# Weights staged through several buffers and idle slots, x loaded a block ahead, the second output product split by k among the next block's columns

## The chip, the cores and the metric

One core of one Trainium2 chip runs the kernel. The metric is the device time of one execution in microseconds (us); lower is better. TensorE is called PE, VectorE DVE, ScalarE ACT, GpSimd POOL and SyncE, which issues every DMA here, SP.

## The reference

A recurrent attention gives `x` (batch 4, 768 positions, 320 features). Two mixtures follow, and they are what the change touches:

```python
def _moe_ref(x, w_in, g_ln, w_sg, b_sg, w_out):
    h = gelu_tanh(x @ w_in)                      # 320 -> 1024
    u, v = h[..., :512], h[..., 512:]
    v_n = (v - mean(v)) / sqrt(var(v) + 1e-06) * g_ln
    v_s = einsum('ts,bsd->btd', w_sg, v_n) + b_sg[None, :, None]   # 768 x 768
    return x + (u * v_s) @ w_out                 # 512 -> 320
def _moe2_ref(x, w_in, conv_w, w_out):
    h = maximum(x @ w_in, 0)                     # 320 -> 1024
    conv_out = three taps of conv_w over the positions of h
    return (h * sigmoid(conv_out)) @ w_out       # 1024 -> 320
```

`w_in` and `w_out` of both mixtures and `conv_w` arrive as 64-bit floats, `w_sg` and the vectors as 32-bit ones.

## The kernel before, in words

`everything` runs `attention`, which writes `x` to a DRAM tensor transposed (features by positions), then `moe`, then a flag that says whether a fallback has to run (it does not here). A scheduler with a timeline of its own turns the order in which the code is written into one order of instructions for each engine; engines run theirs strictly in order. A tile pool gives each name (or tag) a number of buffers, and whoever wants a buffer anew waits until the last reader of the old tile is done.

Every product is made in three terms from a high and a low half of each operand (hi·hi, hi·lo, lo·hi). So each weight is staged: `convert` (L435) loads a piece into the tile `raw` (one buffer, L444), rebuilds 32-bit floats from the 64-bit words with one ACT and four DVE operations into `wq` and `wt` (L448 to L458, which share the tag `vv` with four buffers), and `halves` (L461) writes the high half on ACT and the low half on POOL. `weight_in` (L466) does this in six pieces, left half of the 1024 columns first, `weight_out` (L478) in pieces of 128 rows, `weight_sg` (L509) in six 384 KB pieces that go through the same one buffer.

A block is one batch and one half of the positions, 384 of them; there are eight. First mixture:
- `in1(b, c)` (L522) loads the block's x into `x2t`, splits it into `xh` and `xl`, makes `ph` (the v half, 24 matmuls, L539), gelu, mean and variance and the normalised `vh`, `vl` (L542 to L564), and `pu` (the u half, 32 matmuls, L570).
- `sg(b, c)` (L575) multiplies the `vh`, `vl` of both blocks of a batch by `w_sg`: four groups of 18 matmuls (L588), each finished by DVE `g`, POOL times u, ACT `gh`, DVE `gl`.
- `out1(b, c)` (L600) is the output product, 36 matmuls (L609), written in among the groups of the next `sg`.

They are called in the order of L613 to L628: `in1(0,0)`, all of w_sg, all of w_out, `in1(0,1)`, and then the loop over batches; the second mixture's two weights are staged behind the loop, into the places of the first's (`win_hi`, `big_hi` and their low halves, one buffer each).

Second mixture, after all eight blocks: `in2(i, f)` (L647) makes one of eight columns of 128 hidden features (8 matmuls, L656), and then a chain: ACT relu into `hz` (L657) and first tap into `cv` (L659), DVE the two other taps (L660, L662), ACT sigmoid (L664), POOL times h (L665), ACT `gh` (L668), DVE `gl` (L669). `cv` has two buffers. `out2(i, tt)` (L672) makes one of three groups of 128 positions of the output: 24 matmuls (L679) over all eight columns, evicted by ACT (L682). The loop (L687) writes the three `out2` of block i-1 between the fourth and the fifth column of block i, and the last block's at the end.

Of the kernel before, what the change touches and what calls it, by code (L numbers as in the profile page):

```python
# [10 lines left out]
F32 = mybir.dt.float32  # L11
# [408 lines left out]
def moe(ctx, tc, ident, gy, x, w_in, g_ln, w_sg, b_sg, w_out, w_in2, conv_w, w_out2, out):  # L420
    nc = tc.nc
    B, DM, S = x.shape
    FF = w_in.shape[1]
# [11 lines left out]
    def convert(parts, dst_hi, dst_lo):  # L435

        n = dst_hi.shape[-1]
        m = slice(0, dst_hi.shape[0])
        if parts[0][1].dtype == F32:
            w = work.tile([128, 512], F32, name="raw", bufs=1)  # L440
            for rows, src in parts:
                nc.sync.dma_start(out=w[rows, 0:n], in_=src)
            return halves(w[m, 0:n], dst_hi, dst_lo)
        raw = work.tile([128, 512, 2], U32, name="raw", bufs=1)  # L444
        for rows, src in parts:
            nc.sync.dma_start(out=raw[rows, 0:n], in_=src.bitcast(U32).rearrange("p (n t) -> p n t", t=2))
        low, high = raw[m, 0:n, 0], raw[m, 0:n, 1]
        q = work.tile([128, 512], F32, name="wq", tag="vv", bufs=4)[m, 0:n]  # L448
        t = work.tile([128, 512], U32, name="wt", tag="vv", bufs=4)[m, 0:n]
# [16 lines left out]
    def weight_in(src, name):  # L466

        hi = wpool.tile([128, 3, FF], F32R, name=f"{name}_hi", tag="win_hi")
        lo = wpool.tile([128, 3, FF], F32R, name=f"{name}_lo", tag="win_lo")
        for c in range(0, FF, 512):  # L470
            f = slice(c, c + 512)
            for k in range(3):
                parts = [(slice(0, 128), src[128 * k:128 * k + 128, f])] if k < 2 else \
                    [(slice(0, TAIL), src[256:DM, f]), (slice(64, 128), src[256:DM, f])]
                convert(parts, hi[:, k, f], lo[:, k, f])
        return hi, lo

# [41 lines left out]
    with tc.tile_pool(name="m_u", bufs=9) as pool_u, tc.tile_pool(name="m_wo", bufs=1) as pool_wo:  # L519
        wo = {}  # L520

        def in1(b, c):  # L522
# [6 lines left out]
            xh = work.tile([128, 3, N2], F32R, name="xh", bufs=1)  # L529
            xl = work.tile([128, 2, N2], F32R, name="xl", bufs=1)  # L530
# [44 lines left out]
        def sg(b, c, prev):  # L575
# [3 lines left out]
            for f in range(NF1):  # L579
# [46 lines left out]
        w2_hi, w2_lo = weight_in(w_in2, "w2")  # L626
        out1(*prev)
        v_hi, v_lo = weight_out(wpool, w_out2, NF2, "wv", "big", False)  # L628

    with tc.tile_pool(name="m_g", bufs=2) as pool_g:  # L630
# [16 lines left out]
        def in2(i, f, xh, xl):  # L647
# [10 lines left out]
            cv = work.tile([128, N2], F32, name="cv")  # L658
# [7 lines left out]
            gh = pool_g.tile([128, N2], F32R, name="gh2", bufs=12)  # L666
            gl = pool_g.tile([128, N2], F32R, name="gl2", bufs=12)
# [4 lines left out]
        def out2(i, tt, gs):  # L672
            b, c = divmod(i, 2)
            po = ps_o.tile([128, DM], F32, name="pq", tag="po")
            ts = slice(128 * tt, 128 * tt + 128)
            n = 0
            for g, rr in ((0, v_hi), (0, v_lo), (1, v_hi)):
                for k in range(NF2):
                    nc.tensor.matmul(out=po, lhsT=gs[k][g][:, ts], rhs=rr[:, k], start=(n == 0), stop=(n == 3 * NF2 - 1))  # L679
                    n += 1  # L680
# [88 lines left out]
```

## Time and profile before

| | us |
|---|---|
| median of 3 runs | 1226.54 (1223.62 to 1234.17) |
| span of the profiled execution | 1226.1 |
| PE busy in it | 862.2 (70%) |
| DVE busy | 729.2 (59%) |
| ACT busy | 429.0 (35%) |
| POOL busy | 229.8 (19%) |

The profiled execution has a span of 1226.1 us and stands some 0.4 us under the median of the runs. Attention takes the first 684 us. Busy shares are averages over stages with different limits, so they are read by stretch.

### The profile page before, as it was taken

The numbers are of one execution on the slowest core, as the hardware profiler recorded it, in microseconds if no ns is written. First come the engines' busy times: TensorE is split into PE (matmuls) and PEld (weight loads), VectorE is DVE, ScalarE is ACT, GpSimd is POOL, SyncE is SP. The second block draws the span as 40 slices with busy tenths as digits, with TensorE's granted clock in tenths as the row PEclk, the third lists the DMA queues.
The fourth block names the chain that finished last, engine by engine and source line by source line (L and its number), as shares of the span: only waits on it lengthen the run. The fifth ranks groups of instructions, "written<-read, shape, count | busy, mean of one in ns | idle before, by whom it ended". The sixth has DMA issues, their size and how long they took to land.

```text
span 1226.1 us, 23366 instructions
## 1 busy us (share of the span) xinstructions
PE 862.2 (70%) x9777; PEld 798.7 (65%) x9777; DVE 729.2 (59%) x1348; ACT 429.0 (35%) x833; POOL 229.8 (19%) x217
## 2 busy tenths in 40 slices
PE   2207652973867488296789056599999977999895
PEld 2207642763756477285678045499999966999894
DVE  6573277459459637935932334775555668667663
ACT  2204211321332241133133133232333246767663
POOL 5212010011010201101000023121111424323321
PEclk9657785977879688687989669799999988999997
DMA  9712260244154242413301732100000221000000
GB/s 159 135 33 40 43 113 22 59 78 105 27 106 90 58 75 57 97 44 53 71 22 27 204 118 63 50 1 1 1 1 1 69 71 32 32 18 18 17 32 20
DMA packets 102786, 69.33 MB, mean 57 GB/s; under 512 B 83600, under 2 KB 89744, under 8 KB 101520
## 3 DMA queue, kind: packets, MB, share of 16 engines
q1 hardware_dynamic: 102672, 67.75, 24.9%
q8 instruction: 79, 1.29, 0.5%
q14 instruction: 35, 0.29, 0.1%
HBM read 59.86 MB, written 7.86 MB: 55 GB/s over the span
## 4 chain that ended last, share of the span: by engine, by line
PE 41%; DVE 25%; DMA 16%; issue 6%; ACT 6%; POOL 3%; SPq 1%; DVEq 0%; POOLq 0%; ACTq 0%
PE pv L588 6%; PE gk L124 4%; DVE mtmp L168 3%; PE pr L609 3%; DVE mu L170 3%; PE pq L679 3%; DMA raw<-in_moe_w_in 3%; DMA at<-in_c_a 3%; PE pu L570 3%; PE ph L539 3%; DMA w<-in_c_wp 2%; PE pzt L252 2%; PE gh L276 2%; PE p L656 2%; DMA raw<-in_moe_w_out 2%
## 5 line engine op out<-in xcount | busy, mean ns | idle before, releaser
L189 PE MATMUL pn<-tn,la 32*32 32x32 f32 x768 | 18.9, 214 | 156.9 <-DVE tn L174 155.7
L189 PEld LDWEIGHTS pn<-tn,la 32*32 32x32 f32 x768 | 17.5, 129 | 159.3 <-issue 156.8
L124 PE MATMUL gk<-at,kbt 128*128 128x128 f32 x384 | 68.8, 330 | 45.2 <-POOL kbt L102 31.8
L124 PEld LDWEIGHTS gk<-at,kbt 128*128 128x128 f32 x384 | 60.2, 236 | 48.6 <-POOL kbt L102 32.2
L102 POOL TENSOR_TENSOR kbt<-kbt,w 128x1024 f32<-128x1024 f32 x24 | 55.5, 2330 | 166.6 <-DMA w<-in_c_wp 61.9
L665 POOL TENSOR_TENSOR cv<-cv,hz 128x384 f32<-128x384 f32 x64 | 60.7, 955 | 130.6 <-ACT cv L664 130.6
L100 DVE SCALAR_TENSOR_TENSOR at<-at,px 64x512 f32<-64x512 f32 x48 | 42.3, 916 | 65.8 <-DMA at<-in_c_a 59.7
L168 DVE TENSOR_TENSOR mtmp<-mu 128x30 f32<-128x30 f32 (+9 forms) x180 | 67.0, 372 | 5.0
L170 DVE TENSOR_TENSOR mu<-mu,mtmp 128x30 f32<-128x30 f32 (+9 forms) x180 | 64.8, 360 | 5.0
L539 PE MATMUL ph<-wi_hi,xh 128*128 128x512 f32 x72 | 24.0, 435 | 62.3 <-ACT wi_hi L462 40.0
L588 PE MATMUL pv<-sg_hi,vh 128*128 128x384 f32 x192 | 64.5, 336 | 0.6 <-ACT vh L562 0.6
L588 PE MATMUL pv<-sg_lo,vh 128*128 128x384 f32 x192 | 64.5, 336 | 0.0
L207 ACT ACTIVATE la<-at 64x1024 f32<-64x1024 f32 x24 | 25.2, 1052 | 110.4 <-PE pn L189 63.2
L588 PE MATMUL pv<-sg_hi,vl 128*128 128x384 f32 x192 | 63.8, 336 | 0.0
L592 POOL TENSOR_TENSOR g<-g,u 128x384 f32<-128x384 f32 x32 | 35.5, 1112 | 138.9 <-DVE g L591 136.6
L679 PE MATMUL pq<-wv_hi,gh 128*128 128x320 f32 x192 | 43.8, 334 | 23.9 <-ACT gh L668 23.9
L135 POOL COPY la<-la 32x512 f32<-32x512 f32 x24 | 14.6, 608 | 241.9 <-DVE la L127 219.7
L285 PE MATMUL pyo<-r,s 128*64 128x64 f32 x704 | 57.3, 248 | 3.1 <-ACT n L195 1.9
L280 DVE TENSOR_TENSOR ghs<-gh,mask 128x512 f32<-128x512 f32 x48 | 32.7, 681 | 44.5 <-PE gh L276 26.7
L539 PEld LDWEIGHTS ph<-wi_hi,xh 128*128 128x128 f32 x72 | 14.3, 207 | 67.6 <-ACT wi_hi L462 40.6
L287 PE MATMUL pyo<-ghs,kbn 128*64 128x64 f32 x768 | 57.5, 241 | 0.0
L127 DVE TENSOR_TENSOR la<-gk,mask 128x512 f32<-128x512 f32 x48 | 33.0, 687 | 41.3 <-PE gk L124 41.2
(151 smaller groups left out, 2463.7 us busy)
## 6 DMA issues: line engine op xcount, KB each, us to landing
kbt<-in_c_kb SPq DMA_DIRECT2D x24, 384.0 KB
w<-in_c_wp SPq DMA_DIRECT2D x48, 130.0 KB
w<-in_c_wr SPq DMA_DIRECT2D x48, 130.0 KB
zv<-in_c_vt SPq DMA_DIRECT2D x48, 128.0 KB
at<-in_c_a SPq DMA_DIRECT2D x24, 192.0 KB
r<-in_c_r SPq DMA_DIRECT2D x48, 96.0 KB
raw<-in_moe_w_in SPq DMA_DIRECT2D x8, 512.0 KB
vz<-in_c_v SPq DMA_DIRECT2D x24, 160.0 KB
```

The lines of the kernel that those rows point to most:

```text
L100: nc.vector.scalar_tensor_tensor(out=at[half[P], ns, P], in0=at[half[P], ns, P], scalar=-1.0, in1=px[half[P], ns, 0:C], op0=ALU.mult, op1= ...
L102: nc.gpsimd.tensor_tensor(out=kbt[:, ns], in0=kbt[:, ns], in1=w2[:, :, C - 1::-1][:, :, None, :].to_broadcast([128, 8, 2, C]), op=ALU.mult)
L124: nc.tensor.matmul(out=pg[:, j].rearrange("p P t -> p (P t)"), lhsT=kbt[:, n].rearrange("p c t -> p (c t)"), rhs=at[:, n].rearrange("p P t ...
L168: nc.vector.tensor_tensor(out=tv, in0=mu[:, j + 1:32, j:j + 1].to_broadcast([128, n, j]), in1=mu[:, j:j + 1, 0:j].to_broadcast([128, n, j] ...
L170: nc.vector.tensor_tensor(out=mu[:, j + 1:32, 0:j], in0=mu[:, j + 1:32, 0:j], in1=tv, op=ALU.add)
L285: nc.tensor.matmul(out=pyo[half[P], i], lhsT=s0s[hg, q][:, D * i:D * i + 64], rhs=r2[:, i, P], start=True, stop=False)
L287: nc.tensor.matmul(out=pyo[half[P], i], lhsT=kbn[:, 8 * q + i, P], rhs=ghs[:, j, P], start=(hg == 0), stop=True)
L539: nc.tensor.matmul(out=po, lhsT=xx[:, k, 128 * i:128 * i + 128], rhs=ww[:, k, FH:FF], start=(n == 0), stop=(n == len(ps) - 1))
L570: nc.tensor.matmul(out=po, lhsT=ww[:, k, 128 * f:128 * f + 128], rhs=xx[:, k], start=(n == 0), stop=(n == len(ps) - 1))
L588: nc.tensor.matmul(out=po, lhsT=l[:, fs], rhs=rr[:, k, cs], start=(n == 0), stop=(n == 3 * NT - 1))
L665: nc.gpsimd.tensor_tensor(out=cv, in0=cv, in1=h[:, 1:N2 + 1], op=ALU.mult)
L679: nc.tensor.matmul(out=po, lhsT=gs[k][g][:, ts], rhs=rr[:, k], start=(n == 0), stop=(n == 3 * NF2 - 1))
```

## The change

- The load of a piece (`load`) is parted from its conversion. `raw` has two buffers; the pieces of `w_in` alternate between these and the two buffers of `u`, which are idle then; `w_sg` goes in twelve half pieces through the twelve buffers of `gh` and `gl`.
- `weight_in` takes the right half of the columns (the one that `ph` needs) first.
- The loads of x become `in1_x`, called one block ahead of the block's `in1`.
- `in1(0,1)` is written ahead of the staging of `w_sg` and `w_out`; the second mixture's `conv_w` and `w_in` are staged ahead of the last batch's `sg` instead of behind it.
- `out2` takes one column k (9 matmuls into three accumulators) and is written behind each `in2` of the next block; a new `finish2` evicts the three accumulators. `gh2`, `gl2` go from 12 to 16 buffers.
- `xh`, `xl`, `g`, `gh`, `gl`, the `wo` halves, `cv` and `xt` move to other pools; `g` has two buffers instead of three.

```diff
+    def load(parts, n, pool, bufs, tags):
+
+        if len(parts[0][1]) == 1:
+            w = pool.tile([128, n], F32, name="wst", tag=tags[0], bufs=bufs)
+            for rows, (src,) in parts:
+                nc.sync.dma_start(out=w[rows], in_=src)
+            return [w]
+        raw = pool.tile([128, 512, 2], U32, name="raw", tag=tags[0], bufs=bufs)
+        for rows, (src, _) in parts:
+            nc.sync.dma_start(out=raw[rows, 0:n], in_=src.bitcast(U32).rearrange("p (n t) -> p n t", t=2))
+        return [raw[:, :, 0], raw[:, :, 1]]
...
-    def weight_in(src, name):
+    def weight_in(src, name, slots):
...
-        for c in range(0, FF, 512):
+        for c in (512, 0):
...
+                pool, tag = slots[k % len(slots)]
...
+                convert(load(parts, 512, pool, 2, (tag,)), hi[:, k, f], lo[:, k, f])
...
-        in1(0, 0)
-        weight_sg()
-        wo[0] = weight_out(pool_wo, w_out, NF1, "wo", "wo", True)
+        in1_x(0, 0)
+        wi_hi, wi_lo = weight_in(w_in, "wi", ((work, "raw"), (pool_u, "u")))
+        nc.sync.dma_start(out=g_bc, in_=g_ln[None, :].to_broadcast([128, FH]))
+        in1_x(0, 1)
+        in1(0, 0)
...
         in1(0, 1)
+        for c in range(2):
+            for k in range(NT):
+                cs = slice(N2 * c, N2 * c + N2)
+                raw = load([(slice(0, 128), (w_sg[128 * k:128 * k + 128, cs],))], N2, pool_u, 6, ("gl" if k % 2 else "gh",))
+                convert(raw, sg_hi[:, k, cs], sg_lo[:, k, cs])
+        nc.sync.dma_start(out=b_bc, in_=b_sg[None, :].to_broadcast([128, S]))
+        wo[0] = weight_out(pool_u, w_out, NF1, "wo", "wo", True)
         prev = None
         for b in range(B):
             for c in range(2):
+                if b + 1 < B:
+                    in1_x(b + 1, c)
                 prev = (b, c, sg(b, c, prev))
...
-        w2_hi, w2_lo = weight_in(w_in2, "w2")
+            if b + 2 == B:
...
+                w2_hi, w2_lo = weight_in(w_in2, "w2", ((work, "raw"),))
         out1(*prev)
...
-        def out2(i, tt, gs):
...
+        def out2(k, gs, acc):
+
             n = 0
             for g, rr in ((0, v_hi), (0, v_lo), (1, v_hi)):
...
+                for tt in range(3):
+                    nc.tensor.matmul(out=acc[tt], lhsT=gs[k][g][:, 128 * tt:128 * tt + 128], rhs=rr[:, k],
+                                     start=(k == 0 and n == 0), stop=(k == NF2 - 1 and n == 2))
+                n += 1
...
             xs = start2(i)
-            gs = [in2(i, f, *xs) for f in range(4)]
-            if prev is not None:
-                for tt in range(3):
-                    out2(i - 1, tt, prev)
-            gs += [in2(i, f, *xs) for f in range(4, NF2)]
+            acc = None if prev is None else accumulators()
+            gs = []
+            for f in range(NF2):
+                gs.append(in2(i, f, *xs))
+                if acc is not None:
+                    out2(f, prev, acc)
+            if acc is not None:
+                finish2(i - 1, acc)
             prev = gs
```

Three places in the order of the instructions. The first is SP's queue from the last stores of attention (`x_attn<-xo`) on; `x2t` are loads of x, and each of the first mixture's `raw` is one piece of a weight. Before:

```order
L295 DMA x_attn<-xo 40x4x64 x4
L528 DMA x2t_6062<-x_attn 128x384
L528 DMA x2t_6062<-x_attn 64x384
L446 DMA raw<-in_moe_conv_w 128x48
L528 DMA x2t_6062<-x_attn 64x384
L528 DMA x2t_6062<-x_attn 128x384 x2
L446 DMA raw<-in_moe_w_in 128x1024
L528 DMA x2t_6062<-x_attn 64x384 x2
```

And in the changed kernel (x2t_5978 is batch 0):

```order
L295 DMA x_attn<-xo 40x4x64 x4
L530 DMA x2t_5978<-x_attn 64x384
L622 DMA g_bc<-in_moe_g_ln 128x512
L444 DMA raw<-in_moe_w_in 128x1024 x2
L444 DMA raw<-in_moe_w_in 64x1024 x2
L444 DMA raw<-in_moe_w_in 128x1024
L530 DMA x2t_5978<-x_attn 128x384 x2
L530 DMA x2t_5978<-x_attn 64x384 x2
L440 DMA wst<-in_moe_w_sg 128x384
L444 DMA raw<-in_moe_w_in 128x1024
L440 DMA wst<-in_moe_w_sg 128x384 x9
L444 DMA raw<-in_moe_w_in 64x1024 x2
```

Four of the six pieces of `w_in` are now issued in a row, and `w_sg` between the last two; the x of the other batches, which stood between the pieces, comes behind the first piece of `w_out`.

The second is DVE's queue where the second block's statistics (`bs`, `mv`, the scaled `vv`) and normalisation (`y`, `vl`) stand beside the conversion of `w_out` (the 128x320 `wt`). Before:

```order
L456 SCALAR_TENSOR_TENSOR wt<-raw,wt 128x320
L544 BN_STATS bs<-vv 128x6 x2
L458 SCALAR_TENSOR_TENSOR wt<-wq,wt 128x320
L545 BN_AGGR mv<-bs 128x2 x2
L546 SCALAR_TENSOR_TENSOR vv<-vv,mv,g_bc 128x512 x2
```

The first row is in the last of w_out's four pieces. In the changed kernel:

```order
L565 SCALAR_TENSOR_TENSOR y<-t,y 128x3
L510 TENSOR_TENSOR xl<-x2t_5979,xh 128x768
L511 TENSOR_TENSOR xh<-x2t_5979,xh 64x384
L570 SCALAR_TENSOR_TENSOR vl<-vv,y,vh 128x512 x2
L457 TENSOR_SCALAR wt<-raw 128x320
L570 SCALAR_TENSOR_TENSOR vl<-vv,y,vh 128x512
```

The last row of w_out's staging stood ahead of the second block's statistics; now the first one stands behind them.

The third is ACT's queue in a middle block of the second mixture. `p` is the matmul result of one column. Before:

```order
L659 ACTIVATE cv<-hz_8453,cw 128x384
L668 ACTIVATE gh_9084<-cv 128x384
L659 ACTIVATE cv<-hz_8455,cw 128x384
L664 ACTIVATE cv<-cv 128x384 x2
L668 ACTIVATE gh_9104<-cv 128x384
L659 ACTIVATE cv<-hz_8459,cw 128x384
L668 ACTIVATE gh_9124<-cv 128x384
```

In the changed kernel:

```order
L683 ACTIVATE cv<-hz_8479,cw 128x384
L683 ACTIVATE cv<-hz_8481,cw 128x384
L681 ACTIVATE hz_8473<-p_9405 128x385
L688 ACTIVATE cv<-cv 128x384 x2
L681 ACTIVATE hz_8475<-p_9434 128x385
L692 ACTIVATE gh_9259<-cv 128x384
L681 ACTIVATE hz_8479<-p_9330 128x385
L692 ACTIVATE gh_9288<-cv 128x384
```

Before, a new `cv` starts between the two `gh` of a pair of columns; in the changed kernel both start behind the second one.

## Rows read from the trace of the kernel before

**Rows 1.** By stretch: us, busy PE PEld DVE ACT POOL (instructions), PEclk, DMA share, GB/s

```profile
684.00:700.00 16.00, 0.00 (x0) 0.00 (x0) 5.55 (x12) 3.56 (x7) 1.26 (x1) 0.50 0.81 222
...
789.60:948.20 158.60, 158.60 (x873) 153.71 (x874) 92.82 (x212) 50.20 (x94) 25.95 (x24) 1.00 0.00 1
948.20:980.00 31.80, 31.80 (x185) 31.80 (x184) 22.05 (x37) 9.68 (x17) 12.57 (x10) 1.00 0.21 67
980.00:1003.80 23.80, 15.46 (x70) 13.67 (x68) 14.60 (x31) 7.08 (x14) 7.33 (x13) 0.78 0.26 77
1003.80:1039.30 35.50, 27.30 (x141) 25.64 (x141) 31.04 (x50) 24.69 (x49) 13.93 (x13) 0.92 0.12 38
1039.30:1209.70 170.40, 152.53 (x897) 147.94 (x897) 116.50 (x179) 117.45 (x246) 51.74 (x56) 0.95 0.06 21
1209.70:1226.10 16.40, 9.99 (x51) 9.73 (x51) 0.56 (x1) 1.32 (x3) 0.00 (x0) 0.81 0.11 36
```

**Rows 2.** Timeline, 692 to 727 us: start, duration, engine, instruction, [idle before <- releaser]

```profile
692.07 0.43 DVE L452 TENSOR_SCALAR wt<-raw 128x512 uint32<-128x512 uint32 x1 [1.87 <-DMA raw<-in_moe_w_in]
...
694.02 0.33 SPq L446 DMA_DIRECT2D raw<-in_moe_w_in  x1
...
699.16 0.43 DVE L452 TENSOR_SCALAR wt<-raw 128x512 uint32<-128x512 uint32 x1 [4.41 <-DMA raw<-in_moe_w_in]
...
726.36 0.69 DVE L458 SCALAR_TENSOR_TENSOR wt<-wq,wt 128x512 f32<-128x512 f32 x1
```

**Rows 3.** Timeline of PE, around 780 us

```profile
780.01 1.65 PE L539 MATMUL ph<-wi_hi,xh 128*128 128x512 f32 x3 [17.19 <-ACT vv L542]
...
789.56 0.45 PE L588 MATMUL pv<-sg_hi,vh 128*128 128x384 f32 x1 [0.64 <-ACT vh L562]
```

**Rows 4.** Timeline of DVE: the normalised values of the first block

```profile
745.10 2.80 DVE L563 SCALAR_TENSOR_TENSOR vl<-vv,y,vh 128x512 fp32r<-128x512 f32 x3 [0.79 <-ACT vh L562]
```

**Rows 5.** Chain that ended last: start, duration, engine, tile, line, matmuls; PE at full clock

```profile
835.14 12.48 PE pv L588 x72
847.62 5.48 PE ph L539 x24
853.10 5.58 PE pu L570 x32
...
865.04 6.26 PE pr L609 x36
...
1049.20 4.24 PE p L656 x24
...
1063.14 7.92 PE pq L679 x54
```

**Rows 6.** Timeline of DVE, 957 to 965 us: two successive pieces of the second w_in

```profile
957.39 0.43 DVE L452 TENSOR_SCALAR wt<-raw 128x512 uint32<-128x512 uint32 x1 [2.21 <-DMA raw<-in_moe_w_in]
...
964.11 0.43 DVE L452 TENSOR_SCALAR wt<-raw 128x512 uint32<-128x512 uint32 x1 [2.01 <-DMA raw<-in_moe_w_in]
```

**Rows 7.** Timeline of ACT, 1197 to 1220 us

```profile
1197.16 0.61 ACT L659 ACTIVATE cv<-hz,cw 128x384 f32<-128x384 f32 x1 [0.59 <-DVE gl L669]
...
1203.28 0.61 ACT L659 ACTIVATE cv<-hz,cw 128x384 f32<-128x384 f32 x1 [0.60 <-DVE gl L669]
...
1209.17 0.52 ACT L668 ACTIVATE gh<-cv 128x384 fp32r<-128x384 f32 x1 [0.97 <-POOL cv L665]
...
1219.78 0.44 ACT L682 ACTIVATE xt<-pq 128x320 f32<-128x320 f32 x1 [2.06 <-PE pq L679]
```

**Rows 8.** Timeline of DVE, 1035 to 1039 us: two columns while ACT's order alternates

```profile
1035.72 0.83 DVE L660 SCALAR_TENSOR_TENSOR cv<-hz,cw,cv 128x384 f32<-128x384 f32 x1 [0.68 <-ACT cv L659]
...
1038.35 0.76 DVE L660 SCALAR_TENSOR_TENSOR cv<-hz,cw,cv 128x384 f32<-128x384 f32 x1 [0.68 <-ACT cv L659]
```

**Rows 9.** Timeline of PE, 1020 to 1023 us: a column behind an idle gap

```profile
1019.95 1.13 PE L656 MATMUL p<-x2h,w_hi 128*128 128x386 f32 x3 [2.13 <-ACT hz L657]
...
1022.48 1.00 PE L679 MATMUL pq<-wv_hi,gh 128*128 128x320 f32 x3
```

More of the change, by code (lines that the diff above doesn't have):

```diff
@@ L422, in moe @@
     B, DM, S = x.shape
-    FF = w_in.shape[1]
+    FF = w_in.shape[-1]
     FH = FF // 2
@@ L433, in moe, with convert @@
     ps_o = ctx.enter_context(tc.tile_pool(name="m_pso", bufs=4, space=PSUM))
-    def convert(parts, dst_hi, dst_lo):
-        n = dst_hi.shape[-1]
[L438 to L449, printed above, removed]
+    def load(parts, n, pool, bufs, tags):
[8 more added lines that the diff above has]
+        return [raw[:, :, 0], raw[:, :, 1]]
+    def convert(raw, dst_hi, dst_lo):
+        n = dst_hi.shape[-1]
+        if len(raw) == 1:
+            return halves(raw[0][:, 0:n], dst_hi, dst_lo)
+        low, high = (t[:, 0:n] for t in raw)
+        q = work.tile([128, 512], F32, name="wq", tag="vv", bufs=4)[:, 0:n]
+        t = work.tile([128, 512], U32, name="wt", tag="vv", bufs=4)[:, 0:n]
         w = t.bitcast(F32)
@@ L625, in moe @@
                 prev = None
-        w2_hi, w2_lo = weight_in(w_in2, "w2")
+            if b + 2 == B:
+                convert(load([(slice(0, 128), planes(conv_w, slice(0, 128), slice(0, 3 * NF2)))], 3 * NF2, work, 2,
+                             ("raw",)), cw, None)
+                w2_hi, w2_lo = weight_in(w_in2, "w2", ((work, "raw"),))
         out1(*prev)
-        v_hi, v_lo = weight_out(wpool, w_out2, NF2, "wv", "big", False)
+    cw = cw.rearrange("p (k f) -> p k f", k=3)
+    v_hi, v_lo = weight_out(wpool, w_out2, NF2, "wv", "big", False)
     with tc.tile_pool(name="m_g", bufs=2) as pool_g:
@@ L670, in in2, with finish2, accumulators @@
             return gh, gl
-        def out2(i, tt, gs):
-            b, c = divmod(i, 2)
-            po = ps_o.tile([128, DM], F32, name="pq", tag="po")
-            ts = slice(128 * tt, 128 * tt + 128)
+        def out2(k, gs, acc):
             n = 0
             for g, rr in ((0, v_hi), (0, v_lo), (1, v_hi)):
-                for k in range(NF2):
-                    nc.tensor.matmul(out=po, lhsT=gs[k][g][:, ts], rhs=rr[:, k], start=(n == 0), stop=(n == 3 * NF2 - 1))
-                    n += 1
-            o = work.tile([128, 384], F32, name="xt", tag="g", bufs=3)
-            nc.scalar.activation(out=o[:, 0:DM], in_=po, func=AF.Copy)
-            t0 = N2 * c + 128 * tt
-            nc.sync.dma_start(out=out[b, t0:t0 + 128, :], in_=o[:, 0:DM])
+                for tt in range(3):
+                    nc.tensor.matmul(out=acc[tt], lhsT=gs[k][g][:, 128 * tt:128 * tt + 128], rhs=rr[:, k],
+                                     start=(k == 0 and n == 0), stop=(k == NF2 - 1 and n == 2))
+                n += 1
+        def finish2(i, acc):
+            b, c = divmod(i, 2)
+            for tt in range(3):
+                o = pool_g.tile([128, DM], F32, name="xt", bufs=3)
+                nc.scalar.activation(out=o, in_=acc[tt], func=AF.Copy)
+                t0 = N2 * c + 128 * tt
+                nc.sync.dma_start(out=out[b, t0:t0 + 128, :], in_=o)
+        def accumulators():
+            return [ps_o.tile([128, DM], F32, name="pq", tag="po") for _ in range(3)]
         prev = None
@@ L688, in moe @@
             xs = start2(i)
-            gs = [in2(i, f, *xs) for f in range(4)]
-            if prev is not None:
-                for tt in range(3):
-                    out2(i - 1, tt, prev)
-            gs += [in2(i, f, *xs) for f in range(4, NF2)]
+            acc = None if prev is None else accumulators()
[6 more added lines that the diff above has]
+                finish2(i - 1, acc)
             prev = gs
-        for tt in range(3):
-            out2(2 * B - 1, tt, prev)
+        acc = accumulators()
+        for k in range(NF2):
+            out2(k, prev, acc)
+        finish2(2 * B - 1, acc)
 def everything(tc, given, raw, rest, out):
```

56 lines of the change are left out of this document (28 added, 28 removed).

## Prediction

> **What bounds the kernel now.** I read first the busy time by stretch, with cuts where the work changes [rows 1], then the timelines inside the stretches in which PE idles, and last the chain for the price of each kind of matmul [rows 5]. Attention (up to 684 us) is not touched, and its instructions keep their order. Behind it there are five stretches, each with another limit.
>
> A, 684 to 789.6 us: preparation. PE does nothing up to 700 and waits again later; the longest gap, 17.19 us in front of 780.01, is put down to ACT's `vv` [rows 3]. What stands behind it is the one buffer `raw`. A piece of w_in is read by DVE at 692.07, the next may only be issued at 694.02, and DVE reads it at 699.16: 7.1 us a piece, of which DVE works 0.43 + 3 x 0.69 = 2.5 [rows 2]. In this way come six pieces of w_in, then six of w_sg and four of w_out, and the second block's `vv` is written, and queued, behind them all. The stretch ends when that block's `vh` lets PE go on at 789.56 [rows 3].
>
> B, 789.6 to 1003.8: PE-bound, without any gap up to 980; then PE is busy only 15.46 of 23.80 us, at clock 0.78, while the second mixture's weights are staged [rows 1]. C, 1003.8 to 1039.3: first block of the second mixture, eight columns in 35.5 us, mixed with the rest of that staging. D, 1039.3 to 1209.7: 56 columns in 170.4 us, 3.04 each. PE needs less: 8 matmuls of 4.24/24 and 9 of 7.92/54 us [rows 5] make 1.41 + 1.32 = 2.73 a column. Each column's chain over ACT, DVE and POOL is longer than that, and only two `cv` buffers exist: a pair of columns starts at 1197.16 and the next at 1203.28, 6.12 us [rows 7], where the new `cv` waits for DVE's `gl`. E: behind the last `gh` (1209.69) PE still has 9.99 us of matmuls, and the execution ends 16.4 us after it [rows 1, 7].
>
> **The change part by part.** The sum is made against the profiled span of 1226.1 us.
>
> A. Four pieces of w_in are issued in a row and the queue no longer stops behind each; SP still waits at two places, for the first and the third conversion, and behind these waits stand w_sg and the tail of w_in. Up to that last piece SP has to move 6 pieces x 0.52 + 0.59 (second half of x) + 10 x 0.2 MB of w_sg = 5.7 MB. Such transfers ran at 222 GB/s with the DMA engines 0.81 busy [rows 1], so at most 274: 21 us. From 684 that is 705, 707 with the landing, and DVE has converted it by 710; before this was at 727.05 [rows 2]. From there to the first block's `vl` the old kernel took 18 us (745.10) [rows 4]. The new one has done most of `ph` by then, since the right half of the columns comes first; gelu, statistics, three rounds for the square root and the normalisation remain. I bound this at 8 and 18 and take 13: 723. The second block's split, `ph` and statistics follow behind 32 matmuls of `pv`: 2.7 for the split, 3.5 for what pv covers beyond it, 5.48 for ph [rows 5] and some 7 for the rest, 18.5 (16 to 21, estimates from the first block). So `vh` of the second block comes at 741.5 instead of 789.6: 48 us earlier. By then PE has done less for the third block: 18 ph and 14 pu fewer, 18 x 5.48/24 + 14 x 5.58/32 = 6.5 us. A gives 41.5; with the DMA at 222 GB/s and the upper values 29, with DVE alone as limit and the lower ones 53. w_sg (ACT and POOL, off this path) and w_out (due some 15 us later) are hidden; if w_out came late, PE would wait at its first `pr`. That x is loaded a block ahead I cost at nothing: before, its loads stood among the pieces of the first w_in, long before a later block needs them.
>
> The Trainium skill ("DMA: Bandwidth & Descriptors", Rules for kernel authors) wants at least 1 MiB in one DMA, and the change halves w_sg's pieces to 192 KB. The rows show 0.81 busy and 222 GB/s with pieces of 0.1 to 0.5 MB, some in flight together. By that page's table (138 GB/s at 64 KB) the 2 MB of w_sg would take an estimated 14 us instead of 7, and A would give 34; no row shows such pieces by themselves.
>
> B. From 948.2 PE had 2 x 12.48 + 3 x 6.26 = 43.8 us to do [rows 5] and took 55.6. The loss of 11.8 falls in with pieces that come every 6.7 us [rows 6] and stand in DVE's and ACT's queues ahead of the `g` and `gl` that PE waits for. With two buffers a piece waits less; but DVE's whole work in this stretch (6 pieces x 2.5; 8 of 320 columns x 1.6; sixteen g and gl and nine x2t of 384 columns x 0.52, the last two scaled from the 512 columns of [rows 2]) is some 41 us too, so not all of the loss goes. I take half, 6; bounds 11.8 and -5, if a conversion that waits for its DMA holds `g` up more than now.
>
> C. In DVE's queue all eight conversions of the last weight now come before the first column, and they may write only when the last `pv` is done: eight at some 2.3 us (1.6 of DVE and a wait), less the 6.26 of `pr` beside which they begin, put the first column some 9 us behind the start, but the eight columns then run alone, 2.63 each [rows 8]: 30 instead of 35.5, a gain of 5. Bounds -5 (conversions no faster than now) and 10.
>
> D. PE's waits for `gh` go, since out2 reads the block before. But what is late next is the same chain: `cv` still has two buffers. Where ACT's order alternates (sigmoid, next cv, gh) a column took 2.63 (1035.72 to 1038.35) [rows 8], so PE's 2.73 would decide. In the changed order later blocks start both cv behind the second gh; the durations then add up to 5.7 to 6.2 us a pair, against 6.12 now [rows 7]. I take 2.9 a column as the mean of both patterns: 56 x 2.9 = 162, a gain of 8. Bounds: 2.73 (gain 17) and 3.2 (loss 9).
>
> E. Behind the last `gh` only the 9 matmuls of the last column remain instead of 51, 2 to 3 us with their DVE half, then three evictions of 0.44 and what follows the last eviction now, 5.9 us (1220.2 to 1226.1) [rows 7]: 9.8 instead of 16.4, a gain of 6.6 (5 to 8).
>
> Sum: 41.5 + 6 + 5 + 8 + 6.6 = 67. 1226.1 - 67 = 1159; the median of the runs lies 0.4 above the span, so 1160. The moved tiles (`xh`, `cv`, `wo`) change no duration; where a new address meets an old reader, that reader is `pr` of the last block, which precedes the second mixture anyway.
>
> **The rivals.**
> 1. The second mixture becomes PE-bound: chain and PE interleave as in [rows 8] all the way. For it: early blocks have the alternating order, and PE no longer waits for gh. Against it: the paired order of later blocks. D gives 17 and A perhaps 42: 1151.
> 2. New waits take the place of the old ones in A and B: the staged stream is slowed by SP's two waits, A gives 29; B loses 5, C nothing, D nothing, E 5: 1226 - 29 = 1197. For it: three engines in strict order with conversions ahead of the statistics; against it: DMA and DVE both have slack in A (0.81 and 5.55 of 16 us).
> 3. Slower than before, by PE's clock. PE in D has idle gaps again and again; a column behind a gap of 2.13 us took 2.53 us instead of 1.41, at the lower clock of 1.2 GHz [rows 9, 5]. If the new interleaving, a few matmuls and then a pause, kept PE there, a column would cost 2.53 + 1.32 x 1.8 = 4.9 us, 56 columns 275 instead of 162: 1160 + 113 = 1273. It decides once PE is at that clock for over 67/113, 59%, of D. Against it: granted clock 0.95 in D with PE busy 152.5 of 170.4 us [rows 1], and the work per time rises. The Trainium skill ("TensorE: Matmul & The Clock Gate", A second HAM failure mode: psum-queue depth-cycling) names such a case, PE idling briefly between groups that cycle through PSUM banks; by that rule this rival's time would come out, and the trace agrees only for C, where the clock is 0.92.
> 4. The change doesn't do what it says: the scheduler moves the loads back to where they were. Its order shows otherwise; time as before, 1225.
>
> **How the numbers follow.** Forecast 0.67, rival 1 0.14, rival 2 0.13, rival 3 0.04, rival 4 0.02. Faster by over 1% (which is about what a measurement of this kernel tells from no change): the first three, 0.94; within 1%: 0.02; slower: 0.04. The bounds of A to E added at random give some 25 us to either side of 1160; rival 1 lies inside, rival 2 just outside: 1134 to 1190.
>
> **What would show it.** Right: the second block's first `pv` that needs its `vh` between 730 and 754; PE without a gap from there to the last `pr`; the first column of the second mixture's matmuls near 950; blocks of 23 us; some 10 us behind the last `gh`. Wrong: DVE waiting for `raw` over 3 us a piece; PE idle in front of `pr` for w_out; granted clock under 0.9 in D; pairs of columns longer than 6.2 us.

## The result, and the profile after

The changed kernel takes 1178.63 us (median of 4 runs, 1176.41 to 1181.11) against 1227.07: ratio 0.9598, 95% interval 0.9562 to 0.9634. It is faster by 48 us where 67 were forecast (1160, range 1134 to 1190). The profiled execution has a span of 1179.4.

Busy time of the changed kernel by stretch, columns as in [rows 1]:

```profile
693.00:724.90 31.90, 18.36 (x56) 13.55 (x56) 29.37 (x39) 16.43 (x31) 25.55 (x18) 0.67 0.97 276
...
745.75:969.41 223.66, 214.16 (x1156) 206.66 (x1156) 153.07 (x312) 73.23 (x139) 56.58 (x56) 0.98 0.10 30
...
911.20:969.40 58.20, 48.71 (x253) 47.46 (x252) 51.46 (x82) 20.50 (x39) 24.93 (x26) 0.91 0.32 91
...
969.41:1170.72 201.31, 182.39 (x1080) 176.41 (x1080) 140.98 (x216) 138.94 (x288) 59.54 (x66) 0.98 0.05 18
1170.72:1179.40 8.68, 2.40 (x9) 2.00 (x9) 0.56 (x1) 1.10 (x4) 0.00 (x0) 0.53 0.20 67
1026.50:1050.40 23.90, 22.21 (x133) 21.10 (x132) 17.15 (x25) 15.93 (x35) 6.06 (x7) 1.00 0.06 22
```

These are the preparation; the first mixture from the second block's first `pv`; in it the part in which the second mixture's weights are staged; the second mixture up to its last `gh`; the end; and one block of eight columns. Two readings need no experiment. In 693 to 724.9 DVE is busy 29.37 of 31.9 us and the DMA engines 0.97: PE's 17-us gap of [rows 3] is gone, and two resources are full at once. And a block of columns takes 23.9 us, though PE works only 22.2 of them at full clock.

Timeline of PE in the changed kernel, the starts that follow an idle time:

```profile
693.69 1.65 PE L546 MATMUL ph<-wi_hi,xh 128*128 128x512 f32 x3 [15.72 <-DMA raw<-in_moe_w_in]
...
724.92 0.44 PE L595 MATMUL pv<-sg_hi,vh 128*128 128x384 f32 x1 [0.99 <-ACT vh L569]
...
743.73 1.67 PE L546 MATMUL ph<-wi_hi,xh 128*128 128x512 f32 x6 [1.05 <-ACT xh L509]
...
940.18 0.69 PE L616 MATMUL pr<-gh,wo_hi 128*128 128x384 f32 x1 [3.42 <-ACT gh L602]
...
959.77 0.69 PE L616 MATMUL pr<-gh,wo_hi 128*128 128x384 f32 x1 [2.03 <-ACT gh L602]
...
969.41 0.93 PE L680 MATMUL p<-x2h,w_hi 128*128 128x386 f32 x3 [3.20 <-POOL wv_lo L469]
```

The first row gives the end of attention's last matmul, 693.69 - 15.72 = 677.97; in the old kernel it is 677.07. Profiles of different runs end attention up to 6.5 us apart, so the table counts from this point (us; "ends" is the span's end; e1 to e12 are the experiments below).

| kernel | first vh | second block's vh | first p of mixture 2 | last gh | ends |
|---|---|---|---|---|---|
| before | 67.3 | 111.7 | 326.8 | 532.6 | 549.0 |
| changed | 46.2 | 66.0 | 291.4 | 492.8 | 501.4 |
| e1 four cv | 46.1 | 65.9 | 290.1 | 461.2 | 474.3 |
| e2 by group | 45.7 | 65.4 | 289.5 | 490.7 | 505.2 |
| e3 w_sg low on ACT | 45.4 | 59.5 | 288.7 | 491.3 | 500.2 |
| e4 w2, wv low on ACT | 46.0 | 65.7 | 282.3 | 484.0 | 493.3 |
| e5 one raw | 59.8 | 79.7 | 303.0 | 504.3 | 513.3 |
| e6 in1 behind | 46.3 | 66.0 | 290.7 | 492.1 | 501.2 |
| e7 by group, four cv | 46.4 | 66.2 | 290.5 | 466.5 | 481.7 |
| e8 w2, wv low on DVE | 46.1 | 65.9 | 288.4 | 490.7 | 500.0 |
| e9 w_sg through raw | 42.7 | 57.4 | 288.9 | 490.8 | 499.9 |
| e10 left half first | 57.6 | 68.0 | 293.9 | 496.4 | 505.2 |
| e11 e1 + e8 | 46.5 | 66.2 | 287.8 | 459.1 | 473.2 |
| e12 e11, all low on DVE | 47.1 | 61.3 | 286.0 | 457.2 | 470.5 |

By stretch the change gave 35.4 us up to the first `p` (326.8 to 291.4), 4.5 from there to the last `gh` (205.8 to 201.3) and 7.7 in the end (16.4 to 8.7), 47.6 in all; 0.9 of it is lost again by the later end of attention. A profile is one execution: e1, e2, e6 and e7, which leave the staging of the second mixture as it is, make the first `p` between 289.5 and 290.7, so of a difference to the changed kernel's 291.4 some 2 us can be chance.

### The profile page after: what moved, and what is told of

It is laid out like the page before. It is cut to its first block, busy times and chain, and to the rows that moved or that the text cites. A ratio compares the mean times of both kernels' runs of the same rounds, so it can differ in the third digit from the quotient of the medians.

```text
span 1179.4 us, 23401 instructions
## 1 busy us (share of the span) xinstructions
PE 856.1 (73%) x9777; PEld 793.6 (67%) x9777; DVE 748.6 (63%) x1348; ACT 428.5 (36%) x839; POOL 236.9 (20%) x223
## 4 chain that ended last, share of the span: by engine, by line
PE 43%; DVE 24%; DMA 13%; ACT 7%; issue 7%; POOL 3%; SPq 2%; DVEq 0%; POOLq 0%; ACTq 0%
PE pv L595 6%; PE gk L124 4%; DMA at<-in_c_a 4%; PE ph L546 3%; PE pu L577 3%; DVE mtmp L168 3%; DVE mu L170 3%; PE pr L616 3%; PE p L680 3%; PE pzt L252 3%; PE gh L276 3%; DMA w<-in_c_wp 2%; PE pz L231 2%; DVE cv L686 2%; DMA raw<-in_moe_w_in 2%
## 5 line engine op out<-in xcount | busy, mean ns | idle before, releaser
L124 PE MATMUL gk<-at,kbt 128*128 128x128 f32 x384 | 68.9, 330 | 45.7 <-POOL kbt L102 32.3
L689 POOL TENSOR_TENSOR cv<-cv,hz 128x384 f32<-128x384 f32 x64 | 57.7, 909 | 134.6 <-ACT cv L688 134.6
L693 DVE TENSOR_TENSOR gl<-cv,gh 128x384 fp32r<-128x384 f32 x64 | 40.4, 636 | 33.1 <-ACT gh L692 33.0
L280 DVE TENSOR_TENSOR ghs<-gh,mask 128x512 f32<-128x512 f32 x48 | 32.7, 682 | 44.4 <-PE gh L276 26.7
L131 ACT ACTIVATE kbn<-pkb 128x512 f32<-128x512 f32 x48 | 28.6, 595 | 81.1 <-PE pkb L130 80.6
L684 DVE SCALAR_TENSOR_TENSOR cv<-hz,cw,cv 128x384 f32<-128x384 f32 x64 | 40.7, 644 | 25.5 <-ACT cv L683 25.4
```

Of the source, the lines that this page charges most:

```text
L124: nc.tensor.matmul(out=pg[:, j].rearrange("p P t -> p (P t)"), lhsT=kbt[:, n].rearrange("p c t -> p (c t)"), rhs=at[:, n].rearrange("p P t ...
L684: nc.vector.scalar_tensor_tensor(out=cv, in0=h[:, 1:N2 + 1], scalar=cw[:, 1, f:f + 1], in1=cv, op0=ALU.mult, op1=ALU.add)
L689: nc.gpsimd.tensor_tensor(out=cv, in0=cv, in1=h[:, 1:N2 + 1], op=ALU.mult)
L693: nc.vector.tensor_tensor(out=gl, in0=cv, in1=gh, op=ALU.subtract)
```

## The experiments

In all of them the changed kernel is the base, and 1178.6 the time to compare with; each had the kernel before measured beside it (1228.5 to 1228.9).

**The columns of the second mixture (e1, e2, e7).**

e1, ratio 0.9396 (0.9353 to 0.9438), 1153.53 us:

```diff
-            cv = pool_g.tile([128, N2], F32, name="cv")
+            cv = pool_g.tile([128, N2], F32, name="cv", bufs=4)
```

> The changed kernel with four cv buffers instead of two. Theory 1, the second mixture's middle is held by the chain of a column and by the two cv buffers (23.9 us a block, PE busy only 22.2 to 22.5 of them at full clock): blocks fall to about 22.3 us, the seven blocks from 167.4 to 150 to 157 us, the kernel from 1179 to 1163 to 1168. Theory 2, PE with its many small interleaved groups (or ACT and DVE, each 16.5 us busy a block) sets the pace: the blocks stay within 0.5 us of 23.9 and the kernel within 4 us of 1179.

Timeline of ACT in the changed kernel, with two buffers:

```profile
1039.51 0.62 ACT L683 ACTIVATE cv<-hz,cw 128x384 f32<-128x384 f32 x1 [0.22 <-DVE gl L693]
...
1045.64 0.62 ACT L683 ACTIVATE cv<-hz,cw 128x384 f32<-128x384 f32 x1 [0.97 <-DVE gl L693]
...
1047.41 0.62 ACT L683 ACTIVATE cv<-hz,cw 128x384 f32<-128x384 f32 x1 [0.74 <-DVE gl L693]
```

A pair of columns still takes 1045.64 - 1039.51 = 6.13 us, as in [rows 7] (6.12), and each new `cv` waits for DVE's `gl`, the last reader of the old one. Busy time of e1, from its first `p` to its last `gh`, and to the end:

```profile
965.39:1136.47 171.08, 169.35 (x1043) 168.29 (x1044) 149.70 (x215) 136.50 (x288) 69.54 (x66) 1.00 0.06 21
1136.47:1149.50 13.03, 6.94 (x48) 6.68 (x46) 0.65 (x3) 1.09 (x3) 0.00 (x0) 0.94 0.14 46
```

With four buffers PE is busy 169.35 of 171.08 us at full clock: the columns are PE-bound, 2.67 us each. The gain of 25 us is larger than theory 1 had said (11 to 16). The first block isn't the reason: up to its eighth `gh` it takes 29.2 us from the first `p`, 30.8 in the changed kernel. The other seven take 141.9 instead of 170.5, 20.3 a block where theory 1 had said 21.4 to 22.4, in part because PE leaves more of `out2` for the end. Up to the last `gh` 30.2 us go, and 4.3 come back in the end, where PE still has 48 matmuls instead of 9. Theory 2 is out.

e2 writes the three groups of `out2` back between the columns, as in the old kernel; ratio 0.9635 (0.9601 to 0.9668), 1183.41 us. Its core:

```diff
...
-            for f in range(NF2):
-                gs.append(in2(i, f, *xs))
-                if acc is not None:
-                    out2(f, prev, acc)
...
+            gs = [in2(i, f, *xs) for f in range(4)]
+            if prev is not None:
+                for tt in range(3):
+                    out2(i - 1, tt, prev)
+            gs += [in2(i, f, *xs) for f in range(4, NF2)]
...
```

> The changed kernel with the output product of the second mixture taken back to three groups of 24 matmuls between the fourth and the fifth column, 16 buffers of gh2 and gl2 kept. Theory 1, the split by column brought the end (16.4 to 9.4 us) and hardly anything in the columns, which the cv buffers hold: the end is 16 to 17 us again, a column 2.95 to 3.05 us, the kernel 1186 to 1190. Theory 2, the split did bring the columns more, and something else took it away: a column over 3.1 us, the kernel over 1192.

The columns take 201.2 us without the split and 201.3 with it; only the end differs, 14.4 against 8.7. So the split gave the columns nothing, as theory 1 said. The time came out 3 us under its range, in part because the end is 2 us shorter than in the old kernel even by groups. The two ratios overlap (0.9562 to 0.9634 and 0.9601 to 0.9668), so it is the profiles that show the price of the end, not the medians.

e7 is e2 with four `cv` buffers; ratio 0.9458 (0.9437 to 0.9479), 1161.51 us.

> The output product in three groups of 24 again, with four cv buffers. Theory 1, the buffers alone make the columns PE-bound and the split only shortens the end: the columns up to the last gh take 171 to 177 us, the end 15 to 17 us instead of 13.0, the kernel 1154 to 1160. Theory 2, the split is needed as soon as the chain is faster, since PE waits for gh otherwise: the kernel over 1163.

The time lies between the two ranges. The columns take 176.0 us (e1: 171.1) and the end 15.2 (13.0). The split thus brings 7.1 us in the profiles of e1 and e7, 4.9 of them in the columns, and 5.6 in those of the changed kernel and e2, all of them in the end (medians 8.0 and 4.8): the same edit has two prices, by what else limits the stretch.

**DVE beside POOL (e3, e4, e8).** The low half of a staged weight is a subtraction on POOL. In e3 and e4 ACT writes a copy in its place, and the difference is left out.

e3, ratio 0.9582 (0.9543 to 0.9622), 1179.35 us, for `w_sg`; e4, ratio 0.9539 (0.9505 to 0.9572), 1171.54 us, for the second mixture's two weights:

```diff
...
-            nc.gpsimd.tensor_tensor(out=dst_lo, in0=w, in1=dst_hi, op=ALU.subtract)
+            (nc.scalar.activation(out=dst_lo, in_=w, func=AF.Copy) if lo_on == "act" else nc.gpsimd.tensor_tensor(out=dst_lo, in0=w, in1=dst_hi, op=ALU.subtract))
...
```

> The changed kernel, in which ACT writes a copy of the second mixture's w_in and w_out as their low halves, so that difference is left out for these two weights and POOL has fourteen instructions less beside DVE's staging. Theory 1, the same slowing of DVE beside POOL makes it the limit between 911 and 969 us: the conversions take 2.5 us again, PE's loss of 9.5 us before the second mixture falls under 4, the second mixture starts 5 to 8 us earlier, the kernel takes 1171 to 1175. Theory 2, the strict order of DVE's queue with its waits for pieces is the limit: the start moves by under 2 us, the kernel stays within 3 us of 1179.

Timelines of the changed kernel while two pieces of the second `w_in` are converted, DVE and then POOL:

```profile
921.43 0.69 DVE L459 SCALAR_TENSOR_TENSOR wt<-raw,wt 128x512 uint32<-128x512 uint32 x1
922.16 0.69 DVE L461 SCALAR_TENSOR_TENSOR wt<-raw,wt 128x512 uint32<-128x512 uint32 x1
922.77 0.55 DVE L598 TENSOR_TENSOR g<-pv,b_bc 128x384 f32<-128x384 f32 x1
923.24 1.31 DVE L463 SCALAR_TENSOR_TENSOR wt<-wq,wt 128x512 f32<-128x512 f32 x1
924.47 1.24 DVE L457 TENSOR_SCALAR wt<-raw 128x512 uint32<-128x512 uint32 x1
925.75 1.67 DVE L459 SCALAR_TENSOR_TENSOR wt<-raw,wt 128x512 uint32<-128x512 uint32 x1
...
922.19 1.81 POOL L469 TENSOR_TENSOR w_lo<-wt,w_hi 128x512 fp32r<-128x512 f32 x1 [20.34 <-ACT w_hi L467]
923.96 1.46 POOL L599 TENSOR_TENSOR g<-g,u 128x384 f32<-128x384 f32 x1
925.38 1.48 POOL L469 TENSOR_TENSOR w_lo<-wt,w_hi 128x512 fp32r<-128x512 f32 x1
```

DVE's instructions take about twice as long while POOL is at work, and the slow ones end 0.3 to 0.6 us behind the end of one of POOL's (924.55, 925.71 and 927.42 behind 924.00, 925.42 and 926.86), as if they had waited for it. POOL's own queue isn't the delay: before five of its eight products `g` times u from 912 to 969 POOL stands idle for DVE's `g`, 1.2 to 6.3 us each. Relieved of the subtractions, e4 starts mixture 2 at 282.3 instead of 291.4. Its busy time in the part that answers to 911.2 to 969.4:

```profile
908.90:957.90 49.00, 44.31 (x252) 43.05 (x250) 42.89 (x81) 23.97 (x49) 9.86 (x14) 1.00 0.38 106
```

PE idles 4.7 us there instead of 9.5, and the same matmuls take 44.3 us instead of 48.7, since the granted clock stays full (1.00 for 0.91). Theory 1 holds, with 9.1 us where 5 to 8 were expected (7.2 against the earliest of the runs with the same staging), since the clock's part was left out; the idle time stays a little over the 4 expected.

> The changed kernel, in which ACT writes a copy of w_sg as its low half, so the difference w_sg minus its high half is left out and POOL has twelve instructions less beside DVE's conversion of w_in. Theory 1, DVE is the limit from 693 to 725 us, because its instructions take 1.2 to 1.6 us instead of 0.43 to 0.69 while POOL works: they fall back to 0.4 to 0.7, the first vh comes at 716 to 719 instead of 724.15, and the kernel takes 1171 to 1175. Theory 2, the transfers are the limit (DMA engines 0.97 busy in that stretch): vh comes at 722 to 725, the kernel within 3 us of 1179.

Both numbers are theory 2's: the time is that of the changed kernel, and the first `vh` moved by 0.8 us only (724.5). Yet half of theory 1 shows too: DVE did become free. Busy time of e3, and two rows of its DVE:

```profile
694.20:726.10 31.90, 19.81 (x64) 15.66 (x65) 23.19 (x43) 23.18 (x47) 8.42 (x6) 0.70 0.97 279
...
708.98 0.43 DVE L457 TENSOR_SCALAR wt<-raw 128x512 uint32<-128x512 uint32 x1 [2.06 <-DMA raw<-in_moe_w_in]
...
711.97 1.31 DVE L463 SCALAR_TENSOR_TENSOR wt<-wq,wt 128x512 f32<-128x512 f32 x1 [1.11 <-ACT wq L456]
```

DVE's busy time fell from 29.37 to 23.19 us, and the last piece of `w_in` was then late from DRAM (2.06), and ACT with its added copies (1.11). Transfers and DVE thus stood within a few us of each other as limits. ACT's added work makes this a test of the first only in part.

e8 gives the subtractions of the second mixture's weights to DVE (`lo_on` is "dve"; same values); ratio 0.9565 (0.9549 to 0.9581), 1176.13 us. The kernel has two `cv` buffers; the expectation was written for that, though the label says otherwise.

> The changed kernel, in which DVE instead of POOL makes the low halves of the second mixture's two weights (same values). Theory 1, what costs is POOL working beside DVE, more than the work itself: DVE gets 14 instructions of 0.5 to 0.7 us more (8 us) and loses some 12 us of slowing, the second mixture starts 2 to 6 us earlier, the kernel takes 1173 to 1178. Theory 2, DVE's own work is the limit and the added 8 us stand on the path: the start is later, the kernel takes 1181 to 1188.

Fourteen more instructions on DVE, and mixture 2 starts 3.0 us earlier, 1.1 against the earliest of the runs with the same staging. It isn't later, so theory 2 is out; the gain of theory 1 is small, and the medians (1176.13 and 1178.63) don't tell it from noise.

**What made the preparation shorter (e5, e6, e9, e10).** Each undoes one part.

e5, one `raw` buffer, ratio 0.9729 (0.97 to 0.9758), 1194.56 us:

```diff
-        wi_hi, wi_lo = weight_in(w_in, "wi", ((work, "raw"), (pool_u, "u")))
+        wi_hi, wi_lo = weight_in(w_in, "wi", ((work, "raw"),))
...
-                convert(load(parts, 512, pool, 2, (tag,)), hi[:, k, f], lo[:, k, f])
+                convert(load(parts, 512, pool, 1, (tag,)), hi[:, k, f], lo[:, k, f])
...
```

> The changed kernel with one staging buffer again (raw alone, one buffer, for w_in and w_out of both mixtures; u isn't used for it), everything else as changed. Theory 1, the single buffer was what held the preparation: a piece takes some 7 us again, the first vh comes 6 to 14 us later than the 46.2 us behind attention's last matmul of the changed kernel, the kernel takes 1186 to 1198. Theory 2, the new order (second block ahead of w_sg and w_out, w_sg through its own buffers) carries the gain alone: first vh within 3 us of 46.2, the kernel within 4 us of 1179.

PE in e5:

```profile
698.76 1.65 PE L546 MATMUL ph<-wi_hi,xh 128*128 128x512 f32 x3 [6.81 <-ACT wi_hi L467]
707.63 0.79 PE L546 MATMUL ph<-wi_hi,xh 128*128 128x512 f32 x1 [7.21 <-ACT wi_hi L467]
```

PE waits some 7 us for each piece again, the piece's price in [rows 2]. First `vh` 13.6 us later, end 11.9 later in the profile and 15.9 in the medians: theory 1. The later stretches lose nothing by the one buffer: from the second block's `vh` to the end e5 takes 433.6 us, the changed kernel 435.4.

e6 moves `in1(0, 1)` behind the staging of `w_sg` and `w_out`; ratio 0.9589 (0.9556 to 0.9622), 1178.52 us.

> The changed kernel with the second block's in1 written behind w_sg and w_out again. Theory 1, the buffers carry most of it and this order only a few us: the second block's vh comes 4 to 12 us later than 66 us behind attention's last matmul, PE fills part of it, the kernel takes 1180 to 1188. Theory 2, the order carries it: second vh over 20 us later, the kernel over 1195.

Nothing moved: the second block's `vh` comes at 66.0 in both, and neither theory has that number. In the trace DVE does convert `w_out` ahead of the second block's statistics, but SP's order of loads is the same as in the changed kernel, so the run moves only the conversions of `w_out`. With `w_sg` in buffers of its own, the four pieces of `w_out` fit beside PE's and DVE's other work wherever they are written.

e9 sends the halves of `w_sg` through `raw` (`load(..., work, 2, ("raw",))`); ratio 0.9591 (0.956 to 0.9622), 1177.11 us.

> The changed kernel with the twelve half pieces of w_sg through the two raw buffers instead of the twelve of gh and gl. Theory 1, keeping w_sg out of the shared staging buffers is the larger part of the preparation's gain: w_sg comes behind w_in, piece by piece, and the first matmul with it starts 10 to 25 us later than 47 us behind attention's last matmul; PE uses part of that for the second block, the kernel takes 1186 to 1200. Theory 2, the engines and the transfers set the pace anyhow and w_sg would be there in time: the kernel within 4 us of 1179.

Theory 1 falls, the time is that of theory 2. The first `vh` even comes 3.5 us earlier: `w_sg` is now issued behind `w_in`, so it hardly shares the DMA engines with it, and most of its subtractions on POOL come after the conversion of `w_in`; the run doesn't part the two. PE makes `ph` of the second block in the meantime.

e10 takes the left half of the columns first (`for c in (0, 512)`); ratio 0.9607 (0.9577 to 0.9637), 1179.41 us.

> The changed kernel with the left half of w_in's columns first, as before the change. Theory 1, ph waits for the last three pieces: the first vh comes 4 to 10 us later than 46.2 us behind attention's last matmul, the kernel takes 1182 to 1188. Theory 2, the last pieces arrive so close together that the order of the halves matters little: first vh within 3 us, the kernel within 4 us of 1179.

The first `vh` comes 11.4 us later, more than expected, yet the end only 3.8 us later in the profile, and the medians don't tell the two apart, so theory 1 has the `vh` and theory 2 the time. PE does `pu` while it waits, and has it behind it later. The time of one instruction isn't the time of the stage.

**Versions that beat both kernels (e11, e12).** e11 joins e1 and e8: ratio 0.9374 (0.9346 to 0.9401), 1151.43 us. e12 also makes the low halves of `w_in`, `w_sg` and `w_out` of the first mixture on DVE: ratio 0.9339 (0.9311 to 0.9367), 1147.55 us, 31 us below the changed kernel.

> Four cv buffers and the low halves of the second mixture's weights on DVE instead of POOL (same values). Theory 1, the two gains add: 1153.5 for the buffers, 3 us less for the staging, 1148 to 1152. Theory 2, with PE as the bound of the columns DVE's added work delays the first ones: 1154 to 1160.

> The same with the low halves of all staged weights on DVE. Theory 1, wherever POOL works beside DVE, DVE loses as much as the work would cost it: the preparation up to the first vh keeps its 46.2 us or loses up to 2, the kernel takes 1146 to 1152. Theory 2, in the preparation DVE is the limit and the added 18 instructions of 0.55 to 0.7 us stand on the path: the first vh is 4 to 10 us later, the kernel 1154 to 1160.

The times are those of theory 1 in both, and in e12 the first `vh` (47.1) too. That e12 lies below the changed kernel is clear of noise; what e11 gives over e1, and e12 over e11, is not (the ratios overlap). DVE's groups in the preparation, by shape; first the changed kernel, 693 to 724.9 us, mean ns behind the busy time:

```profile
L463 DVE SCALAR_TENSOR_TENSOR wt<-wq,wt 128x512 f32<-128x512 f32 x5 | 6.7, 1333 | 0.4
L461 DVE SCALAR_TENSOR_TENSOR wt<-raw,wt 128x512 uint32<-128x512 uint32 x5 | 6.5, 1300 | 0.2
L457 DVE TENSOR_SCALAR wt<-raw 128x512 uint32<-128x512 uint32 x4 | 3.6, 900 | 0.4 <-DMA raw<-in_moe_w_in 0.3
```

and e12, 690 to 724 us, with the busy time of the stretch as last row:

```profile
L469 DVE TENSOR_TENSOR sg_lo<-wst,sg_hi 128x384 fp32r<-128x384 f32 x12 | 6.1, 552 | 1.8 <-ACT sg_hi L467 1.8
L463 DVE SCALAR_TENSOR_TENSOR wt<-wq,wt 128x512 f32<-128x512 f32 x6 | 4.1, 682 | 0.0
L469 DVE TENSOR_TENSOR wi_lo<-wt,wi_hi 128x512 fp32r<-128x512 f32 x6 | 4.1, 678 | 0.0
L457 DVE TENSOR_SCALAR wt<-raw 128x512 uint32<-128x512 uint32 x5 | 2.1, 421 | 1.2 <-DMA raw<-in_moe_w_in 1.2
...
690.30:724.10 33.80, 20.64 (x63) 15.90 (x64) 28.38 (x61) 19.08 (x35) 0.00 (x0) 0.68 0.95 266
```

DVE does eighteen subtractions more (10.2 us) and is busy 28.38 us (of 33.8) instead of 29.37 (of 31.9): POOL's help had cost DVE as much as it took off it.

## Why the prediction was right or wrong

The direction and the size within a third were right: 48 us came, 67 were said. Part by part, in the profiles' own times:

- **A, said 41.5, measured 37.3.** The step on the time of the second block's `vh` came out: 741.5 was said, 743.95 came (0.9 of it from attention), and PE goes on at 745.75 instead of 789.56, 43.8 us earlier. The step on the PE work that this leaves for later was right to the matmul, 18 `ph` and 14 `pu`, 6.5 us. Busy time by tile from that point to the first `p`, for `ph` and then `pu`, each time before and changed (PE's busy time, behind x the number of matmuls):

```profile
789.56:1003.87 214.31, 28.22 (x120) 0.98 0.06 19
745.75:969.41 223.66, 33.31 (x138) 0.98 0.10 30
789.56:1003.87 214.31, 31.62 (x176) 0.98 0.06 19
745.75:969.41 223.66, 34.25 (x190) 0.98 0.10 30
```

That the first block's `vl` was ready at about the time said (723 was said, 724.90 came) is luck, since two errors cancel:

```profile
714.98 1.31 DVE L463 SCALAR_TENSOR_TENSOR wt<-wq,wt 128x512 f32<-128x512 f32 x1
...
724.90 2.08 DVE L570 SCALAR_TENSOR_TENSOR vl<-vv,y,vh 128x512 fp32r<-128x512 f32 x3 [0.79 <-ACT vh L569]
```

The conversion of `w_in` ends at 716.29 and not at 710, and from there it takes 8.6 us instead of 13. Wrong were the slack that was given to DVE (29.37 of 31.9 us busy) and POOL's work on `w_sg` as off the path: without it DVE is busy for 23.19 us (e3). It hurt little, as the transfers were as full. The cause that was named, one buffer with 7.1 us a piece, is shown by e5 for 13.6 us, all of them ahead of the first `vh`. Of the 45.7 us by which the second `vh` comes earlier in the table, 24.6 lie between the two `vh` (44.4 before, 19.8 now), and none of e5, e6, e9 and e10 brings these back, so what carries them isn't shown. I think that `w_sg` in its own buffers and the second block ahead of `w_sg` stand in for each other, since either alone suffices (e6 writes `in1(0, 1)` behind, e9 takes the buffers away); both undone together wasn't tried, nor were the loads of x a block ahead undone.

- **B, said 6, measured -2.8.** From the second block's `pv` to the first `p` PE stands idle for 9.5 us of 223.7 here and for 8.4 of 214.3 before. A further 1.7 us is longer busy time for the same matmuls; the lower clock is a part of that (0.91 from 911.2 to 969.4, where e4 at full clock needs 4.4 us less, against 0.78 from 980 to 1003.8 before), the rest isn't accounted for. The step that failed is the price of a conversion, 2.5 us of undisturbed DVE, and with it the half of the loss that was to go. DVE's groups by shape, before in 948 to 1003.8 us and changed in 912 to 969.4:

```profile
L452 DVE TENSOR_SCALAR wt<-raw 128x512 uint32<-128x512 uint32 x6 | 2.7, 445 | 10.7 <-DMA raw<-in_moe_w_in 10.7
...
L458 DVE SCALAR_TENSOR_TENSOR wt<-wq,wt 128x320 f32<-128x320 f32 x3 | 1.5, 492 | 0.3
...
L457 DVE TENSOR_SCALAR wt<-raw 128x512 uint32<-128x512 uint32 x6 | 5.0, 833 | 2.9 <-DMA raw<-in_moe_w_in 2.9
...
L463 DVE SCALAR_TENSOR_TENSOR wt<-wq,wt 128x320 f32<-128x320 f32 x6 | 4.5, 749 | 0.2
```

With two buffers DVE waits 2.9 us for the pieces of `w_in` instead of 10.7, but it converts them back to back, just while POOL makes low halves, at 1.2 to 1.7 us for many an instruction. So it is busy 51.46 us of the 58.2 where 41 had been counted: the wait for the DMA has become a wait for DVE. e4 shows it: without POOL's subtractions some 7 to 9 us come back. And e5 shows that the second buffer itself gave these stretches nothing. Part of the loss is only moved here from C: six of the last weight's eight pieces are converted ahead of the first `p`, before it was three.

- **C, said 5, measured 4.6; D, said 8, measured nothing.** The eighth `gh` of the second mixture, before and changed:

```profile
1038.73 0.52 ACT L668 ACTIVATE gh<-cv 128x384 fp32r<-128x384 f32 x1 [0.42 <-POOL cv L665]
...
999.72 0.51 ACT L692 ACTIVATE gh<-cv 128x384 fp32r<-128x384 f32 x1
```

The first block ends 30.8 us behind the first `p` instead of 35.4; 30 was said. That is partly luck too: eight conversions of 2.3 us less 6.26 make 12 and not 9, and most of them were done before that `p`. The 56 columns behind it take 170.5 us, before 170.4: 3.04 each. That the chain with two `cv` buffers would be late next was right; the step that failed in D is the 2.9 a column, the mean of two patterns. The alternating order brings some columns at 2.6 us, as it did before, and most still come in pairs, 5.9 to 6.1 us each. So the waits for `gh` that went were worth nothing in the columns (e2). Price of the buffers by e1: 30 us up to the last `gh`.

- **E, said 6.6, measured 7.7.** Right: nine matmuls remain instead of 51, and e2 gives 5.7 of it back.

Of the signs that were named, the time of the second block's `pv` (745.75), a granted clock over 0.9 and the short end came; PE without a gap up to the last `pr` and a first column near 950 (969.41) did not.

Rival 1 (PE-bound columns) had about the right price of a column (2.73; e1 has 2.67) and the wrong condition: the alternating order of ACT doesn't bring it, more buffers do. Rival 2 (new waits in A and B, 1197) had the loss in B and the nothing in D right and was too low for A, C and E; 1178.6 lies midway between it and the forecast. Rival 3 did not come: the granted clock is 0.98 from the first `p` to the last `gh`. Rival 4 is excluded by the rows above. The estimate from the Trainium skill ("DMA: Bandwidth & Descriptors", Measured) that `w_sg` in small pieces would take 14 us instead of 7, worked out from the table's value for 64 KB, a third of such a piece, wasn't borne out either: 276 GB/s flow in 693 to 724.9, above the 222 of [rows 1].

## What to carry to other kernels

When a transfer wait goes, look at who converts what arrives, and at what runs beside it then: price the instructions as they are with that neighbour, not alone. Before spreading a product over time, check whether the chain that feeds it is held by a buffer count; here two more buffers of one small tile gave 25 us, half as much as the whole change. And parts that stand in for each other would show nothing when undone one at a time, so undo them in pairs before crediting one; here that is still open.

## What the runs showed of the hardware

DVE and POOL disturb each other far more than I had counted: a conversion step of 0.68 to 0.69 us took 1.2 to 1.7 beside POOL, and the shift (L457) 0.9 on average instead of 0.42. Who begins first matters: the step at 922.16 kept its 0.69, and POOL's subtraction that began 0.03 us behind it took 1.81 instead of 1.48. DVE's `g` (L598), which reads one operand from PSUM, kept its 0.55 us beside POOL (922.77). The Trainium skill ("SBUF — State Buffer", Who interferes with whom) states that a DVE instruction with two SBUF inputs contends with a GpSimd one that reads SBUF, that one with a single SBUF input does so only in its two-port modes, and that the pair is locked for a whole instruction. The rows agree for L459 to L463 and for `g`; for L457, with one input, they agree if it runs in such a mode, which no row shows. Had I weighed this rule, the half of the loss in B that was to go would have had no ground.
